# Seven token tiles of 512 and 768 instead of nine of 512

## The chip, the cores and the metric

One core of a Trainium2 chip runs the whole program. The metric is the device time of one execution in microseconds (us), and three runs of the kernel before are at hand. TensorE (PE) multiplies, VectorE (DVE) and ScalarE (ACT) work element by element, GpSimd (POOL) mainly issues stores here, and SyncE's queue (SP) issues the loads.

## What is computed

Linear attention without a mask, a norm over each head's 64 outputs, and a feed-forward layer on all tokens, in float32:

```python
kv = np.einsum('bhsd,bhse->bhde', k, v)            # 8 batches, 8 heads, 576 rows, 64 wide
out = np.einsum('bhsd,bhde->bhse', q, kv)
rms = np.sqrt(np.mean(out * out, axis=-1, keepdims=True) + 1e-06)
x = out / rms * g_norm                             # then 4608 tokens x 512
h = x @ w_in                                       # 512 -> 2048
sp = np.where(h > 20.0, h, np.log1p(np.exp(np.minimum(h, 20.0))))
g = h * np.tanh(sp)                                # Mish
y = g @ w_out                                      # 2048 -> 512
```

## The kernel before

**Numbers.** Each float32 operand of a large product is split into a rounded high part and a rest (`split`: a ScalarE cast, then a VectorE subtraction). A product is three matmuls: high by high, high by rest, rest by high.

**Products.** Both large products use a scheme of seven products on 2 x 2 blocks (a Strassen form, `PROD`). For x @ w_in the blocks are halves of the tokens of a tile, of the 512 inputs and of the 2048 outputs. `x_sum` makes the sums and differences of blocks of x, `x_form` splits the seven left operands ("forms") into fixed rooms, which the products of one tile read and the next tile overwrites.

**Part one.** The 4608 tokens are cut into nine tiles of 512 (`BLOCKS`, `TS`, `OFF`). Tile 0 is multiplied plainly (`whole_group`, line 734), with matmuls of up to 512 columns. Tiles 1 to 8 each have `NQ` = 4 groups, and a group works on two of the eight 128-row chunks of outputs (`chunks`). A group is seven products (slots), and `mm_in` (line 780) gives a product 2 chunks x 2 contraction halves x 3 = 12 matmuls of 256 columns (`TH`). Results lie in PSUM banks "a" and "bc", two of each. ScalarE copies a bank to a room of `u` (`take`, lines 681, 686, 694), the bank is accumulated further two products or more later, VectorE adds it to the copy (`put_in`, line 836), ScalarE applies Mish (line 197), and GpSimd's queue stores g to a DRAM scratch `gd` (line 818), one tensor per tile.

**Attention.** The x of tile j is made while tile j - 1 is multiplied: query loads (452), 32 x 32 transposes on VectorE (470), projection by the key-value product (862, product at 371), squares, sums of squares (532), a table load, logarithm and exponential (542 to 550), a trip of the row scales through DRAM (`keep` 567, `spread` 574) and `normalize` (584).

**w_out.** It comes as raw words; 16 pieces are loaded (224), scaled and joined (215, 210 to 212), differenced and stored to a scratch (`weight_out`), three pieces per tile from tile 2 on. They use two rooms `w64` and two rooms `wx`.

**Part two.** From the last tile's end on, slabs of 256 tokens are loaded from `gd` (`g_load`, 1075), formed, multiplied by w_out (line 1267 for the first slab, 1148 for the others: per product eight matmuls of 512 columns and eight of 256) and stored.

**Order.** Nothing is scheduled automatically. `start(j)` counts slots from tile 0 on, `at(t, f)` puts a step at a slot, and the tables `WHEN`, `LATER` and `LATER0` hold a fractional slot for each step of the attention, the weights and the forms; `LAST` holds those of the change to part two. Steps are emitted in the order of these numbers, and each engine and each queue then works in that order.

Of the kernel before, what the change touches and what calls it, by code (L numbers as in the profile page):

```python
# [8 lines left out]
F32 = mybir.dt.float32  # L9
# [27 lines left out]
def linear_attention_rms_mish_ffn(  # L37
# [47 lines left out]
    TM = max(TS)  # L85
    assert sum(TS) == NTOK
# [12 lines left out]
    def start(j):  # L99
        return FIRST + NS * (j - 1) if j else 0  # L100
    WHEN = {
# [33 lines left out]
    }  # L135
    LATER = {
        "k0": -9, "k1": 0.4878, "k2": 0.2698, "k3": -4, "load0": -20.266, "transpose0": -7.3665,
        "load1": -0.8834, "square0": 1.8552, "scaled0": 1.9552, "transpose1": -0.6728, "square1": 2.0552,
        "scaled1": 2.828, "sums": 5.7127, "table": 6.2457, "ln": 6.6987, "exp": 7.5047, "keep": 7.8047,
# [8 lines left out]
    }  # L148
    LATER0 = {
        "k0": -7, "k1": -2.3472, "k2": -1.299, "k3": -2, "load0": -11, "transpose0": -6, "load1": -5.5,  # L150
        "square0": 5.1305, "scaled0": 0.3, "transpose1": -1, "square1": 0.4, "scaled1": 2.5, "sums": 5.4106,
        "table": 6.6923, "ln": 6.7866, "exp": 7.9866, "keep": 9.0209, "spread": 9.5515, "normalize0": 16.16,
        "normalize1": 17.5, "sum0": 21.4, "sum1": 21.65, "sum2": 22.05, "x0": 25.516, "x1": 25.5, "x2": 26.541,
        "x3": 26.568, "x4": 27.5, "x5": 27.8, "x6": 30.1, "project": 0, "kp": 5.05, "kk": 6,
    }
    LAST = {
# [464 lines left out]
    def x_form(j, f):  # L621

        if j < T32:
            x_sum(j, f)
# [744 lines left out]
```

## Time and profile before

| | |
|---|---|
| median of 3 runs | 808.5 us (807.41 to 808.59) |
| profiled execution, its own time | 809.48 us |
| its span, first to last instruction | 807.7 us |
| mean granted TensorE clock | 0.996 |
| TensorE, VectorE, ScalarE, GpSimd busy | 97%, 74%, 55%, 13% |
| moved by DMA | 158 MB, mean 196 GB/s |

The span is what the trace shows; about 1.8 us of the time lie around it. Durations are in us or ns as marked. A matmul's recorded duration contains pipelining, so that neighbouring matmuls overlap; the distance between the starts of equal matmuls is what one costs in a stream.

### The profile page before, as it was taken

What the parts mean: (1) busy time and instruction counts of PE and PEld (TensorE: products, weight loads), DVE (VectorE), ACT (ScalarE), POOL (GpSimd) and SP (SyncE); (2) the same over time, 40 slices, a digit from 0 to 9 for tenths busy, and PEclk for the clock granted to TensorE, in tenths of its full rate; (3) what the DMA queues carried; (4) which work ended last, traced back from release to release, by engine and by line L of the source; (5) the groups of instructions that cost most, each with busy time, mean ns of one, the idle gap of its engine ahead of it and who ended that gap; (6) DMA issues with size and microseconds to landing.
All of it is one profiled execution on the core that took longest, in us unless ns stands there. A gap on an engine that the chain in (4) does not pass through costs nothing.

```text
span 807.7 us, 16677 instructions
## 1 busy us (share of the span) xinstructions
PE 785.2 (97%) x6764; PEld 716.5 (89%) x6764; DVE 595.2 (74%) x795; ACT 445.4 (55%) x688; POOL 108.5 (13%) x195
## 2 busy tenths in 40 slices
PE   6899999999999988999999999999999999999998
PEld 5777899899999988998999998888888888888887
DVE  3897858575766847676446888888888888878885
ACT  4858776547465754746457654444444444444442
POOL 2210111322322333332111100000000000000000
PEclk9999999999999999999999999999999999999999
DMA  8998468694959757772479923343333334344422
GB/s 294 287 325 245 169 201 290 183 350 130 329 212 290 245 171 241 217 277 102 158 273 337 353 107 131 143 144 130 131 131 131 131 131 141 136 143 143 148 74 54
DMA packets 65453, 158.00 MB, mean 196 GB/s; under 512 B 9184, under 2 KB 29920, under 8 KB 63072
## 3 DMA queue, kind: packets, MB, share of 16 engines
q1 hardware_dynamic: 51136, 109.93, 41.8%
q0 software_dynamic: 14144, 46.93, 15.5%
q8 instruction: 53, 0.87, 0.4%
q14 instruction: 24, 0.20, 0.1%
q10 hardware_dynamic: 96, 0.07, 0.0%
HBM read 100.40 MB, written 56.49 MB: 194 GB/s over the span
## 4 chain that ended last, share of the span: by engine, by line
PE 89%; DMA 4%; DVE 3%; ACT 2%; issue 1%; SPq 1%; ACTq 0%; DVEq 0%
PE a L1148 23%; PE a L780 22%; PE bc L1148 18%; PE bc L780 16%; PE q L1267 2%; DMA w<-in_moe_w_in_dram 2%; PE x L862 2%; PE x L371 2%; DMA fh<-rd 1%; PE a L734 1%; PE x L532 1%; PE bc L734 1%; DMA wfb<-in_moe_w_in_dram 1%; DVE gf L584 0%; PE x L734 0%
## 5 line engine op out<-in xcount | busy, mean ns | idle before, releaser
L200 ACT CAST gf<-g 128x1024 fp32r<-128x1024 f32 (+1 forms) x103 | 105.9, 1044 | 96.1 <-PE a L1148 50.6
L201 DVE TENSOR_TENSOR gf<-g,gf 128x1024 fp32r<-128x1024 f32 (+1 forms) x103 | 123.7, 1214 | 43.9 <-ACT gf L200 43.9
L780 PE MATMUL a<-gf,wfb 128*128 128x256 f32 x1152 | 151.0, 285 | 2.0 <-DVE u L836 2.0
L780 PEld LDWEIGHTS a<-gf,wfb 128*128 128x128 f32 x1152 | 144.3, 194 | 4.2 <-DVE u L836 2.4
L1148 PE MATMUL a<-wfb,gf 128*128 128x512 f32 (+1 forms) x800 | 144.9, 337 | 0.0
L1148 PEld LDWEIGHTS a<-wfb,gf 128*128 128x128 f32 x800 | 125.4, 190 | 16.4
L1148 PE MATMUL bc<-wfb,gf 128*128 128x512 f32 (+1 forms) x544 | 98.0, 337 | 0.0
L1148 PEld LDWEIGHTS bc<-wfb,gf 128*128 128x128 f32 x544 | 82.6, 190 | 10.1
L818 POOL DMA_DIRECT2D gd<-u x96 | 57.1, 597 | 221.1 <-ACT u L197 181.5
L197 ACT ACTIVATE u<-u 128x1024 f32<-128x1024 f32 (+1 forms) x65 | 54.8, 844 | 45.9 <-DVE u L836 45.4
L836 DVE TENSOR_TENSOR u<-bc,u 128x512 f32<-128x512 f32 x64 | 43.3, 687 | 33.5 <-PE bc L780 30.4
L780 PE MATMUL bc<-gf,wfa 128*128 128x256 f32 x384 | 51.8, 284 | 1.3 <-DVE gf L201 0.9
L780 PEld LDWEIGHTS a<-gf,wfa 128*128 128x128 f32 x384 | 48.3, 192 | 5.0 <-issue 4.2
L780 PE MATMUL a<-gf,wfa 128*128 128x256 f32 x384 | 51.9, 284 | 0.0
L780 PE MATMUL bc<-gf,wfb 128*128 128x256 f32 x384 | 51.4, 283 | 0.0
L780 PE MATMUL bc<-a,wfb 128*128 128x256 f32 x384 | 51.4, 283 | 0.0
L780 PEld LDWEIGHTS bc<-gf,wfa 128*128 128x128 f32 x384 | 48.4, 192 | 2.4 <-DVE gf L201 1.1
L1148 PE MATMUL bc<-wfa,gf 128*128 128x256 f32 (+1 forms) x272 | 50.3, 337 | 0.0
L1148 PEld LDWEIGHTS a<-wfa,gf 128*128 128x128 f32 x272 | 44.1, 189 | 6.6
L1148 PE MATMUL a<-wfa,gf 128*128 128x256 f32 (+1 forms) x272 | 49.8, 336 | 0.0
L200 ACT CAST gf<-a 128x1024 fp32r<-128x1024 f32 x17 | 17.9, 1055 | 57.0 <-DVE a L1092 57.0
L780 PEld LDWEIGHTS bc<-a,wfb 128*128 128x128 f32 x384 | 48.4, 192 | 0.6 <-issue 0.6
(203 smaller groups left out, 1183.8 us busy)
## 6 DMA issues: line engine op xcount, KB each, us to landing
g<-gd SPq DMA_DIRECT2D x18, 2048.0 KB
gd<-u POOLq DMA_DIRECT2D x72, 256.0 KB, 4.8
gd<-u POOLq DMA_DIRECT2D x36, 512.0 KB, 6.0
w<-in_moe_w_out_dram SPq DMA_DIRECT2D x32, 256.0 KB
km<-in_k_dram SPq DMA_DIRECT2D x28, 288.0 KB
vm<-in_v_dram SPq DMA_DIRECT2D x28, 288.0 KB
wfb<-in_moe_w_in_dram SPq DMA_DIRECT2D x28, 256.0 KB
out_dram<-u SPq DMA_DIRECT2D x44, 128.0 KB
```

The source lines that it names most:

```text
L197: nc.scalar.activation(o, i, AF.Mish)
L200: nc.scalar.copy(hi, src)
L201: nc.vector.tensor_sub(lo, src, hi.bitcast(F32))
L371: nc.tensor.matmul(outs[a][half(o, a == 1)], kt[half(o), d], vt[half(o), d], start=(c == 0), stop=(c == 8))
L532: nc.tensor.matmul(ss[j][hp * R:(hp + 1) * R, c], sel, sq[j, n][:, a, c], start=True, stop=True)
L734: nc.tensor.matmul(bank[:, h], w[:, a, kc, :], xf[:, h, b, kc, :], start=new and kc == p == 0, stop=(second == 1 and hs[-1] == 1 and kc == ...
L780: nc.tensor.matmul(bank[:, jj], w[:, a, kc, :], xf[:, b, kc, :], start=first and jj == kc == s == 0, stop=(kc == 1 and s == 2), skip_group ...
L818: eng.dma_start(to, o)
L836: nc.vector.tensor_add(o, bank, o)
L862: nc.tensor.matmul(x2[half(o), a, cols], kvt[b % 2][r, m, u], of[r, c, m], start=m == 0, stop=m == 1)
L1148: nc.tensor.matmul(to, of, by, start=first and n == 0, stop=n == len(todo) - 1, skip_group_check=True)
L1267: nc.tensor.matmul(banks[b][:, h], gf[:, a, c, :], wo_form(2 * n + c, right)[:, :, d, :], start=n == c == s == h == 0, stop=last_one, skip ...
```

## The change

Part one has seven tiles: three of 512 tokens and four of 768. Attention runs on parts (`SUBS`): the first three parts are tiles 0 to 2, and then each tile of 768 has two parts of 384 (`TILES`, `HOME`), each with its own steps ("a" and "b" in the tables). In the tiles of 768 a group works on one chunk of outputs instead of two, so that a tile has eight groups and a product six matmuls of 384 columns, in one PSUM bank. All slot numbers in the tables are new. w_out pieces are placed five to a tile over tiles 3 to 5, and the sixteenth after them.

Rooms change with the sizes: the forms' rooms are one tensor (`homes`), `u` is 7 x 384 wide, key and value loads have two rotating rooms and some borrowed ones, `wx` has one room, and one of the two `ow` rooms of part two lies in the room of x. Before the first load of weights its room is now filled with zeros on GpSimd (`clear`). `gd` has rows of 384 in the large tiles, so that a slab there is read in pieces of 256 or 128 tokens per chunk; slabs 0 and 1 are read in four parts each (`g00` to `g13`).

```diff
-    BLOCKS = (16,) * 9
-    NT = len(BLOCKS)
-    TS = [32 * n for n in BLOCKS]
+    SUBS = (512,) * 3 + (384,) * 8
+    TILES = ((0,), (1,), (2,)) + tuple((j, j + 1) for j in range(3, 11, 2))
+    NT = len(TILES)
+    HOME = {j: (i, h if len(js) > 1 else None) for i, js in enumerate(TILES) for h, j in enumerate(js)}
+    SO = [sum(SUBS[:j]) for j in range(len(SUBS))]
+    TS = [sum(SUBS[j] for j in js) for js in TILES]
...
     LATER = {
+        "aload0": -6, "aload1": -5.5, "atranspose0": 3, "atranspose1": 4, "aproject": 5.2, "asquare0": 7.5042,
...
+        "akp": 8.2372, "akk": 14.4383, "asums": 9.5756, "atable": 10.1517, "aln": 10.3517, "aexp": 11.5292,
+        "akeep": 11.7292, "aspread": 12.0958, "anormalize0": 20.8936, "anormalize1": 23.4848, "bload0": 10.3183,
...
+        "bln": 31.5, "bexp": 31.8, "bkeep": 32, "bspread": 33.2, "bnormalize0": 39.266, "bnormalize1": 41.4583,
+        "sum0": 43.3923, "sum1": 45.5101, "sum2": 47.189, "x0": 52.8317, "x1": 52.6366, "x2": 56.3748,
+        "x3": 54.3298, "x4": 56.5377, "x5": 56.9798, "x6": 61.0377, "wload0": 7.7085, "wscale0": 15.8522,
+        "wjoin0": 17.267, "wdiff0": 19.9101, "wblocks0": 20.377, "wforms0": 21.0305, "wstore0": 21.0922,
+        "wload1": 21.2416, "wscale1": 25.1154, "wjoin1": 26.0084, "wdiff1": 26.6154, "wblocks1": 28.0444,
+        "wforms1": 28.1154, "wstore1": 29.2011, "wload2": 27.9154, "wscale2": 33.6, "wjoin2": 34.6151,
+        "wdiff2": 35.1, "wblocks2": 35.366, "wforms2": 36.4421, "wstore2": 36.7421, "wload3": 35.766,
+        "wscale3": 42.3923, "wjoin3": 45.4163, "wdiff3": 45.8813, "wblocks3": 45.9149, "wforms3": 47.1078,
...
+        "wforms4": 65.5, "wstore4": 66.5319, "wload5": 62.5, "wscale5": 67.5, "wjoin5": 69.4963,
...
+        def clear():
+            st["t"] = room()
+            st["w"] = st["t"].rearrange("p b n t -> p (b n) t")
+            nc.gpsimd.memset(st["t"].bitcast(F32), 0.0)
...
+    def bank_of(n, two):
+        def new(name):
+            bank = bank_new(name)
+            return bank[:, :, 0:n] if two else bank.rearrange("p m t -> p (m t)")[:, 0:n].rearrange("p (m t) -> p m t", m=1)
+        return new
...
-        open_pools(wst, ("w64", 2), ("wx", 2), ("wst", 1))
-    at(start(1) + 18, out_pools)
+        open_pools(wst, ("w64", 2), ("wx", 1), ("wst", 1))
+    at(start(3) + 13, out_pools)
...
-        j, n = 2 + min(i, 14) // 3, i % 3 if i < 15 else 3
+        j, n = 3 + min(i, 14) // 5, i % 5 if i < 15 else 5
...
-    def g_load(s):
-        g = gs[s]["g"] = pools["gp"].tile([P, NFC, G], F32, name="g")
-        nc.sync.dma_start(g, gd[s // 2][:, s % 2])
+    def g_load(s, n=None):
...
+        for i in range(NT):
+            th = TS[i] // 2
+            for h in range(2):
+                at_ = OFF[i] + h * th
+                lo, hi = max(at_, s * G), min(at_ + th, (s + 1) * G)
+                if lo < hi:
+                    to, of = g[:, :, lo - s * G:hi - s * G], gd[i][:, h, :, lo - at_:hi - at_]
...
+                    nc.sync.dma_start(to, of)
...
-        for n in range(NQ):
-            st = {"i": i, "n": n, "chunks": (2 * n, 2 * n + 1), "bank": bank_new, "take": nc.vector.tensor_copy if T32 <= i < NT - 1 and n in BY_DVE else nc.scalar.copy}
+        two = i == 0 or TS[i] < TM
+        for n in range(NQ if two else NF2):
+            st = {"i": i, "n": n, "chunks": (2 * n, 2 * n + 1) if two else (n,), "bank": bank_new if i == 0 else bank_of(TS[i] // 2, two), "take": nc.scalar.copy}
```

## Rows read from the trace of the kernel before

**Rows 1.** The page, busy time of each engine with its share of the span and its instructions:

```profile
PE 785.2 (97%) x6764; PEld 716.5 (89%) x6764; DVE 595.2 (74%) x795; ACT 445.4 (55%) x688; POOL 108.5 (13%) x195
```

**Rows 2.** Stretches of the span: start and end, length, then for PE, PEld, DVE, ACT and POOL the busy time with its instructions, the granted clock, the DMA engines' share, GB/s. The start, two windows of the 512-token tiles, part two:

```profile
0.00:36.00 36.00, 27.69 (x286) 22.09 (x287) 18.93 (x34) 22.22 (x41) 8.11 (x31) 0.95 0.90 300
...
184.00:232.00 48.00, 48.00 (x572) 46.19 (x572) 32.85 (x53) 29.35 (x49) 12.57 (x21) 1.00 0.77 255
...
280.00:328.00 48.00, 43.13 (x508) 40.36 (x507) 31.34 (x57) 25.81 (x47) 16.79 (x25) 0.96 0.63 208
...
472.00:805.00 333.00, 332.01 (x1914) 293.05 (x1912) 272.15 (x265) 152.79 (x187) 0.00 (x0) 1.00 0.36 123
```

**Rows 3.** The same view for the matmuls of line 780 alone (PE, then PEld), from the start of tile 3 to the end of tile 8:

```profile
178.90:455.00 276.10, 247.11 (x2018) 244.18 (x2017) 0.99 0.69 234
```

**Rows 4.** Timeline of TensorE at the end of tile 0: start, duration to the end of the last, instructions, tile shape and count:

```profile
73.44 2.88 PE L734 MATMUL a<-gf,wfb 128*128 128x512 f32 x12
76.16 2.88 PE L734 MATMUL bc<-gf,wfb 128*128 128x512 f32 x12
78.88 2.88 PE L734 MATMUL a<-gf,wfb 128*128 128x512 f32 x12
81.60 2.88 PE L734 MATMUL bc<-gf,wfb 128*128 128x512 f32 x12
84.32 1.59 PE L780 MATMUL a<-gf,wfb 128*128 128x256 f32 x12
```

**Rows 5.** The chain that ended last, in a tile of part one and in a slab of part two: start, share of the chain, what:

```profile
209.18 2.88 PE bc L780 x24
...
505.67 5.56 PE a L1148 x32
```

**Rows 6.** Groups of instructions by line and shape: count, busy us, mean ns of one, idle before them and what ended it. Copies, Mish, casts, adds, subtractions, the table load and the stores of g:

```profile
L201 DVE TENSOR_TENSOR gf<-g,gf 128x1024 fp32r<-128x1024 f32 x102 | 123.2, 1221 | 43.4 <-ACT gf L200 43.4
L200 ACT CAST gf<-g 128x1024 fp32r<-128x1024 f32 x102 | 105.5, 1050 | 96.1 <-PE a L1148 50.6 <-DVE g L1097 31.1 <-DVE g L1095 14.4
...
L818 POOL DMA_DIRECT2D gd<-u x96 | 57.1, 597 | 221.1 <-ACT u L197 181.5 <-issue 13.1 <-ACT kv L393 6.4
...
L836 DVE TENSOR_TENSOR u<-bc,u 128x512 f32<-128x512 f32 x64 | 43.3, 687 | 33.5 <-PE bc L780 30.4 <-ACT u L197 1.5 <-ACT fa L503 1.2
...
L197 ACT ACTIVATE u<-u 128x1024 f32<-128x1024 f32 x32 | 34.0, 1062 | 8.8 <-DVE u L836 8.3
...
L200 ACT CAST gf<-gf 128x512 fp32r<-128x512 f32 x36 | 21.8, 620 | 1.8 <-PE a L780 1.2 <-DVE gf L584 0.6
L197 ACT ACTIVATE u<-a 128x512 f32<-128x512 f32 x35 | 21.1, 602 | 1.6 <-DMA gd<-u 1.6
...
L681 ACT COPY u<-a 128x512 f32<-128x512 f32 x32 | 18.7, 585 | 30.9 <-PE a L780 29.3 <-ACT gf L200 1.5
...
L542 ACT ACT_TABLE_LOAD x8 | 10.3, 1283 | 0.1
```

**Rows 7.** Stretches again (columns as in rows 2): the last group of tile 2, in which the forms of tile 3 are made:

```profile
168.90:179.00 10.10, 10.10 (x87) 10.10 (x86) 6.33 (x11) 6.84 (x12) 2.65 (x5) 1.00 0.97 325
```

**Rows 8.** Stretches again: tile 4, then tile 5, from first product to first product of the next tile:

```profile
224.85:270.79 45.94, 45.94 (x555) 44.13 (x554) 32.50 (x55) 28.02 (x48) 11.07 (x19) 1.00 0.76 252
270.79:324.15 53.36, 48.49 (x554) 45.83 (x553) 35.25 (x61) 30.65 (x54) 19.45 (x29) 0.97 0.62 205
```

**Rows 9.** Timeline of TensorE in tile 5; in brackets the idle time before and what ended it:

```profile
285.02 0.45 PE L371 MATMUL x<-vm,km 64*64 64x64 f32 x13 [2.58 <-issue]
...
313.93 2.41 PE L780 MATMUL a<-gf,wfb 128*128 128x256 f32 x10 [1.77 <-DVE u L836]
```

**Rows 10.** The chain that ended last, at the entry to tile 1 and in tile 5: start, share, what:

```profile
74.63 4.68 DMA fh<-rd
...
299.92 5.67 DMA fh<-rd
```

**Rows 11.** What SP's queue waited for between 270 and 320 us: total us, times, longest:

```profile
SPq L224 <- DMA wod<-w: 24.2, 3, 13.3
```

**Rows 12.** What the engines waited for over the whole span, the normalize line: total us, times, longest:

```profile
DVE gf L584 <- DMA fh<-rd: 7.2, 5, 2.4
```

**Rows 13.** Timeline of ScalarE (the exponential of tile 1's row scales), then of SP's queue (their store and the spread):

```profile
70.21 0.63 ACT L550 ACTIVATE fl<-fl 128x512 f32<-128x512 f32 x1
...
70.87 1.18 SPq L567 DMA_DIRECT2D rd<-fl  x4
...
73.96 1.28 SPq L574 DMA_DIRECT2D fh<-rd  x2
```

**Rows 14.** Timeline of the first us: GpSimd's memsets and loads, and the first weight load on SP's queue:

```profile
1.28 0.20 POOL L913 MEMSET wfa<- 128x128 f32 x1
...
1.95 0.14 POOL L917 MEMSET sel<- 128x32 f32 x1
...
2.31 1.38 SPq L242 DMA_DIRECT2D w<-in_moe_w_in_dram  x2
2.33 1.20 POOL L925 DMA_DIRECT2D gcol<-in_g_norm_dram  x2
```

**Rows 15.** DMA issues by kind: count, KB each, median us from issue to landing. Stores that read a `w64` room and a `wx` room:

```profile
wod<-w POOLq DMA_DIRECT2D x16, 256.0 KB, 3.2
...
wod<-wx POOLq DMA_DIRECT2D x16, 128.0 KB, 3.8
```

More of the change, by code (lines that the diff above doesn't have):

```diff
@@ L148, in linear_attention_rms_mish_ffn @@
     }
     LATER0 = {
[L150 to L154, printed above, removed]
+        "aload0": -14, "aload1": -12.6004, "atranspose0": -6.6293, "atranspose1": -4.5, "aproject": -3.5,
@@ L381, in linear_attention_rms_mish_ffn @@
     open_pools(wst, ("w64", 1), ("wd", 1))
-    first = fq.tile([P, 2 * TM], F32, name="a22")[:, 0:2 * NKC * D].rearrange("p (s n d) -> p s n d", s=2, d=D)
+    first = spare[:, 0:2 * NKC * D].rearrange("p (s n d) -> p s n d", s=2, d=D)
     kvn, kvy = first[:, 0], first[:, 1]
@@ L525, in sums @@
                 return
-            if j >= T32:
-                ss[j] = x2_new()[:, 0]
-                for c in (slice(0, T),):
-                    for n in range(2):
-                        for a in range(2):
-                            hp = 2 * n + a
-                            nc.tensor.matmul(ss[j][hp * R:(hp + 1) * R, c], sel, sq[j, n][:, a, c], start=True, stop=True)
-                return
-            ss[j] = ps_t.tile([P, T], F32, name="ss")
+            ss[j] = x2_new()[:, 0, 0:tj]
             for n in range(2):
@@ L603, in x_rows, with x_home @@
     def x_rows(j, u):
-        return x_of(j).rearrange("p h a n -> p a h n")[:, 2 * u:2 * u + 2]
-    def x_sum(j, f):
-        a11, a12, a21, a22 = block(j, 0, 0), block(j, 1, 0), block(j, 0, 1), block(j, 1, 1)
-        n = TS[j]
+        i, h = HOME[j]
+        if h is None:
+            return x_of(i).rearrange("p h a n -> p a h n")[:, 2 * u:2 * u + 2]
+        return x_of(i)[:, h, 2 * u:2 * u + 2]
+    PAIRS = ((A11, A21), (A12, A22), (S1, S2))
+    def x_home(f):
+        pair = next(n for n, p in enumerate(PAIRS) if f in p)
+        n = PAIRS[pair].index(f)
+        return homes[:, (4 * pair + 2 * n) * TM:(4 * pair + 2 * n + 2) * TM]
@@ new lines, in x_sum @@
+    def x_sum(i, f):
+        a11, a12, a21, a22 = block(i, 0, 0), block(i, 1, 0), block(i, 0, 1), block(i, 1, 1)
+        n = TS[i]
+        if n == TM:
+            room = att.tile([P, 2 * T], F32, name={S1: "fa", S2: "fh", S4: "fl"}[f])
+        else:
+            if f == S1:
+                xsums[i] = pools["wd"].tile([P, 4, 2 * P], F32, name="wd").rearrange("p a n -> p (a n)") if i == 2 else x_room
+            room = spare if f == S2 else xsums[i]
+        xsums[i, f] = room[:, 0:n].rearrange("p (c n) -> p c n", c=2)
@@ L785, in linear_attention_rms_mish_ffn, with u_room @@
     held = []
-    u_all = up.tile([P, 7 * T], F32, name="u")
     u_uses = {}
-    def u_room(name, small, n):
-        first, size, bufs = {
-            ("la", False): (0, T, 2), ("lb", False): (2 * T, T, 1), ("r", False): (3 * T, 2 * T, 2),
-            ("la", True): (0, TM // 2, 3), ("lb", True): (3 * TM // 2, TM // 2, 2), ("r", True): (3 * T, TM, 3),
-        }[name, small]
-        k = u_uses[name, small] = u_uses.get((name, small), -1) + 1
+    def u_room(name, i, n):
+        k = u_uses[name] = u_uses.get(name, -1) + 1
+        if name == "o":
+            return u_all[:, k % 2 * 2 * T:][:, 0:n]
+        if TS[i] < TM:
+            if "more" not in u_uses:
+                u_uses["more"] = pools["w64"].tile([P, 4, 2 * P, 2], U32, name="w64").rearrange("p a b c -> p (a b c)").bitcast(F32)
+            more = u_uses["more"]
+            room = {
+                ("la", 0): u_all[:, 2 * T:], ("la", 1): more[:, 3 * T:], ("lb", 0): more[:, 2 * T:], ("lb", 1): more[:, 2 * T:],
+                ("r", 0): u_all, ("r", 1): more,
+            }[name, k % 2]
+            return room[:, 0:n]
+        first, size, bufs = {"la": (0, TF, 2), "lb": (2 * TF, TF, 1), "r": (3 * TF, TM, 2)}[name]
         return u_all[:, first + k % bufs * size:][:, 0:n]
@@ L840, in put_in @@
             done(right, st["r"], None, 3, 2)
-    units = {j: [unit_steps(j, u) for u in range(2)] for j in range(NT)}
+    units = {j: [unit_steps(j, u) for u in range(2)] for j in range(len(SUBS))}
     def do(j, u, *steps):
@@ L979, in linear_attention_rms_mish_ffn @@
         at(t, steps[name])
-    def soon(j, name):
-        return (LATER0 if j == 2 else LATER)[name]
-    for b in range(4, B):
-        t = start(b - 2)
-        at(t + soon(b - 2, "kp"), lambda b=b: k_product(b))
-        at(t + soon(b - 2, "kk"), lambda b=b: k_keep(b))
-        for p in range(4):
-            at(t + soon(b - 2, f"k{p}"), lambda b=b, p=p: k_load(b, p))
+    KP = {3: 4, 5: 5, 6: 6, 8: 7}
     def attention(j):
+        i, h = HOME[j]
+        t, table = start(i - 1), LATER0 if i == 3 else LATER
         def spread():
@@ L994, in spread @@
             units[j][1]["spread"]()
-        units[j][0]["spread0"] = spread
-        t = start(j - 1)
         def when(name, f):
-            at(t + soon(j - 1, name), f)
+            at(t + table["ab"[h] + name], f)
         for u in range(2):
@@ L1007, in attention @@
         when("spread", spread)
-        for n, f in enumerate((S1, S2, S4)):
-            when(f"sum{n}", lambda f=f: x_sum(j, f))
-        for n, f in enumerate(MADE):
-            when(f"x{n}", lambda f=f: x_form(j, f))
-    for j in range(3, NT):
+        if j in KP:
+            b = KP[j]
+            when("kp", lambda: k_product(b))
+            when("kk", lambda: k_keep(b))
+            for p in range(4):
+                when(f"k{p}", lambda p=p: k_load(b, p))
+        if h:
+            for n, f in enumerate((S1, S2, S4)):
+                at(t + table[f"sum{n}"], lambda f=f: x_sum(i, f))
+            for n, f in enumerate(MADE):
+                at(t + table[f"x{n}"], lambda f=f: x_form(i, f))
+    for j in range(3, len(SUBS)):
         attention(j)
@@ L1179, in o_store @@
                 at_ = st["s"] * G + r * P + n * R
-                i = max(i for i in range(NT) if OFF[i] <= at_)
-                b, s0, seg = next(e for e in segments(i) if e[2].start <= at_ - OFF[i] < e[2].stop)
-                runs.setdefault((i, b), []).append((r, b * S + s0 + (at_ - OFF[i] - seg.start) // R, (seg.stop - seg.start) // R))
+                j = max(j for j in range(len(SUBS)) if SO[j] <= at_)
+                b, s0, seg = next(e for e in segments(j) if e[2].start <= at_ - SO[j] < e[2].stop)
+                runs.setdefault((j, b), []).append((r, b * S + s0 + (at_ - SO[j] - seg.start) // R, (seg.stop - seg.start) // R))
             for rs in runs.values():
@@ L1206, in pair_rooms @@
         if n == 0:
-            return [pools["g0"].tile([P, m, 2, 2, P], F32R, name=f"g{m}") for m in (4, 3)]
-        return [gf_room() for _ in range(2)]
+            a, b = [pools["g0"].tile([P, m, 2, 2, P], F32R, name=f"g{m}") for m in (4, 3)]
+            return [(a, b)[f // 4][:, f % 4] for f in range(7)]
+        at_ = {
+            1: {A11: 0, S1: 4, A12: 8, A22: 12, S2: 24, S3: 28, S4: 32},
+            2: dict(zip(range(7), (16, 20, 36, 40, 44, 48, 52))),
+            3: dict(zip(range(7), range(56, 84, 4))),
+        }[n]
+        return [homes[:, at_[f] * P:(at_[f] + 4) * P].bitcast(F32R).rearrange("p (s c n) -> p s c n", s=2, c=2) for f in range(7)]
     t8 = start(NT - 1)
@@ L1213, in linear_attention_rms_mish_ffn @@
     for s in range(2):
-        at(t8 + LAST[f"g{s}"], lambda s=s: g_load(s))
+        for n in range(NQ):
+            at(t8 + LAST[f"g{s}{n}"], lambda s=s, n=n: g_load(s, n))
     rooms0 = {}
```

171 lines of the change are left out of this document (85 added, 86 removed), and 87 rows, old and new, of tables (LAST, LATER, WHEN).

## The prediction

> **What bounds the kernel now.** I read the totals first: TensorE is busy for 785.2 of 807.7 us, and VectorE and ScalarE stand at 74% and 55% [rows 1]. Busy shares alone don't decide, so the stretches come next. In the stage of the 512-token tiles TensorE is busy for all 48.00 of 48.00 us at a granted clock of 1.00, and in the second half of the kernel for 332.01 of 333.00 [rows 2]; VectorE and ScalarE have 15 to 19 us of slack in such a 48 us window. TensorE is therefore the bound, and a change pays there only by giving it fewer or shorter instructions, or by removing a stall. One stall is large: the window 280 to 328 has only 43.13 busy and a clock of 0.96 [rows 2]. The start is different: up to 36 us the DMA engines are 90% busy at 300 GB/s [rows 2], and TensorE idles for 8.3 us.
>
> **What a matmul costs.** The recorded duration (283 ns) overlaps its neighbours, so I take distances between starts. In the chain 24 matmuls of 256 columns take 2.88 us: 120.0 ns each [rows 5]. In tile 0 twelve matmuls of 512 columns start every 2.72 us (73.44, 76.16, 78.88, 81.60, 84.32): 226.7 ns each [rows 4]. The line through both has 0.4168 ns per column, 2.4 GHz, and 13.3 ns per matmul whatever its width. For 384 columns it gives 173.3 ns. A second reading: in the second half 32 matmuls, half of 512 and half of 256 columns, take 5.56 us [rows 5], so 512 columns are 227.5 and 384 are 173.8.
>
> **The change part by part.**
>
> *Matmuls.* Tiles 3 to 8 of before hold 6 x 4 x 7 x 12 = 2016 matmuls of 256 columns (2018 in their window, edges included [rows 3]). After, the same tokens are 4 tiles x 8 groups x 7 products x 6 = 1344 matmuls of 384 columns: the same columns, 672 fixed parts fewer. 2016 x 120.0 = 241.9 us; 1344 x 173.3 = 232.9. **-9.0 us** (-8.4 by the second reading), all of it on the path. The Trainium skill (TensorE: Matmul & The Clock Gate, Back-to-back issue gap) gives an isolated warm matmul N/2.4 + 2.5 ns: by that only 672 x 2.5 = 1.7 us would be won, an estimate that speaks against the change. The trace disagrees: 120.0 ns at 256 columns is 13.3 over the columns' own time, so I keep -9.0.
>
> *The stall in tile 5.* Tile 4 takes 45.94 us and tile 5, with one TensorE instruction less, 53.36 [rows 8]: 7.4 us lost. TensorE waits 2.58 us inside the key-value product and 1.77 us for the add of line 836 [rows 9]; the lower clock after these holes is the rest. Its cause is in SP's queue: the w_out load of line 224 waits up to 13.3 us for a room whose stores haven't landed [rows 11], the spread of line 574 stands behind it, and the normalize of line 584 waits for that transfer, 5.67 us in the chain [rows 10], with the adds behind it. The diff places every one of these steps anew (w_out pieces five to a tile over tiles 3 to 5, loads 7 to 23 slots apart, a slot now 6 x 173.3 = 1.04 us). Between a piece's store and the load that takes its room again lie at least 6.6 slots, 6.9 us, against 3.2 us from issue to landing of such a store [rows 15] and three to five issues of some 0.6 us. I count the stall as gone: **-7.4 us** (0 if it comes back).
>
> *Less cover for each eviction.* A product lasts 1.04 us instead of 1.44, so the two products between an accumulator's copy and its next use shrink from 2.88 to 2.08 us. Per group, with sizes scaled between rows 6: ScalarE 3 copies of 478 ns, two Mish of 495 and one of 847, 3.3 us; VectorE 3 adds of 554, 1.7 us; the group lasts 7.28. In general that fits. At the entry to a 768 tile it doesn't: seven casts of 835 ns bring ScalarE to 9.1 us, seven subtractions of 954 ns bring VectorE to 8.3, where before a whole such group used 6.84 and 6.33 of 10.1 us [rows 7]. The cover: each form has 6 products, 6.2 us, between its last use and its next, and needs about 1.9, so 4 us of lag are free. If that cover were gone, the excess of 1.8 us would reach TensorE at the three entries whose last group is already of 384 columns: 0 to 5.5. I take half, **+2.7**.
>
> *The spread.* From the end of the exponential to the arrival of the first spread rows the trace has 70.84 to 79.31, 8.5 us [rows 10, 13]. Planned now: 9.36 slots (9.7 us) in a tile's first part, but 7.47 slots (7.8 us) in its second, 0.6 of which is the exponential itself. So four normalizes are about 1.3 us late, and the adds queue behind each on VectorE. Even before, five such waits came to 7.2 us [rows 12]. 0 to 5.2, half of it hidden by the 2.08 us: **+2.6**.
>
> *One wx room instead of two.* ScalarE's scale of a w_out piece now waits until the stores that read the last piece have landed: two issues of 0.6 us and 3.8 us to landing [rows 15], 5 us. The plan leaves 4.1 slots (4.3 us) for the second piece of a tile, 5.3 and more for others, and 2 slots for the last piece. Behind the scale on ScalarE stand the copies that TensorE needs. Late by 0.7 three times and 2.9 once, 0 to 5: **+1.7**.
>
> *Attention in eight parts of 384 instead of six of 512.* Batch borders cut both into 11 pieces, so projections, query loads and their DMAs stay equal. Two more pairs of table loads (1283 ns each [rows 6]) fall on ScalarE, eight more row-scale stores and eight more spreads on SP, 24 more stores of 597 ns [rows 6] on POOL's queue, which was 13% busy [rows 1]. Hidden: 0.
>
> *Start.* A memset of 2048 columns now precedes the first weight load. Memsets of 32 and 128 columns took 0.14 and 0.20 us [rows 14]: some 1.5 us, from about 3.5 to 5.0, and SP's first weight load moves from 2.31 to 5.0, with what is queued behind it. The 1.7 MB of query, key and value ahead of it keep the DMA engines full for some 5.5 us at 300 GB/s, so I take 0; +2.7 if that cover fails, -1.5 if the keys come sooner for it.
>
> *g scratch in four parts, rows of 1 KB or 512 B instead of 16 KB (16 chunks x 256 tokens x 4 bytes).* The second half moves a mean 123 GB/s at a DMA share of 0.36 [rows 2]: 0.
>
> **Sum** against the profiled execution's 809.5 us (span 807.7): 809.5 - 9.0 - 7.4 + 2.7 + 2.6 + 1.7 = 800.1. The median of the runs, 808.5, is 1.0 lower, so the forecast is **799 us**.
>
> **The rivals.**
> - *No new stall.* The tables place each step apart, and the window 184 to 232 of before ran without one [rows 2]. The last three terms vanish, the start may give 1.5: 790.6 to 793. Against it: the shorter slots.
> - *In-order queues become the bound; slower.* Place: ScalarE and VectorE in the 32 groups of 384 columns. ScalarE had 29.35 of 48 us busy, VectorE 32.85 [rows 2], with four groups, one attention part and three w_out pieces in about that time. With eight smaller groups, two smaller parts and five pieces I estimate about 51 us each in some 65 us (58.2 of products and 7 of attention): 78%, in queues where a copy stands behind a cast or a table load. It decides from 16.4 us of new stalls, 0.51 us per group. At 0.7 per group, 22.4 us: 814.5.
> - *The tile-5 stall comes back at full size elsewhere*, by SP's order: 799 + 7.4 = 806.4.
> - *The change doesn't shorten the matmuls.* If the fixed part grew with width, 384 columns would cost 180 ns and the term would be 0: 808. Rows 4 speak against it (512 would be 240). By the gap that the Trainium skill states (same section) 1.7 us would be won, 806.3.
>
> **How the numbers follow.** Forecast, 795 to 804, 0.52; no new stall 0.18; slower queues 0.13; stall back 0.12; no shorter matmuls 0.05. A measurement of this kernel tells 0.2%, 1.6 us, from no change: faster is below 806.9, slower above 810.1. Faster 0.52 + 0.18 + 0.07 + 0.02 = 0.79; same 0.04 + 0.03 = 0.07; slower 0.13 + 0.01 = 0.14. The range runs from the full gain, 790, to 809, which takes in the returned stall and the unshortened matmul and leaves out the slower case and little below: some 0.83. The likeliest case alone has 795 to 804: 3.5 to 12 us of new stalls out of 15.7 at most.
>
> **What would show it.** Right: 384-column matmuls in the 768 tiles, 6 in 1.04 us; a tile of about 58.2 us plus some 7 to 8 us of attention; full TensorE in windows inside a tile; holes of 0.3 to 2 us only at tile entries, at line 584's counterpart and behind the scale of w_out pieces. The second half stays at 333 us and the first 84 us within 3. Wrong: 384 columns at 180 ns; TensorE holes in most groups, released by the adds or copies; a clock below 1.00 in the 768 tiles; a later first matmul.

## The result, and the profile after

The changed kernel is slower: a median of 816.8 us (815.0 to 819.1, four runs) beside 808.6 us of the kernel before, timed with it, a ratio of 1.0103 (95% interval 1.0067 to 1.0139). The forecast was 799 us, faster. The profiled execution took 819.08 us with a span of 817.3; it is the slowest of the four, so the losses read from it below are at the upper end.

The totals show little. Busy times of the page, then stretches (columns as in [rows 2]): a window of the first 768-token tile, one that covers most of the third and the start of the last, and part two.

```profile
PE 788.6 (96%) x6108; PEld 709.2 (87%) x6108; DVE 595.1 (73%) x809; ACT 457.4 (56%) x737; POOL 125.0 (15%) x220
...
184.00:232.00 48.00, 45.24 (x577) 39.44 (x576) 23.81 (x41) 24.78 (x45) 10.73 (x18) 0.93 0.71 228
...
345.00:420.00 75.00, 67.58 (x384) 62.74 (x384) 47.82 (x85) 40.53 (x75) 30.91 (x50) 0.96 0.66 218
472.00:805.00 333.00, 333.00 (x1938) 294.87 (x1937) 274.54 (x268) 157.38 (x194) 0.00 (x0) 1.00 0.43 130
```

Part two is as before [rows 2]. Tile 1 starts at 84.27 us (84.32 before), part two's first slab at 460.45 (450.40 before). So tiles 1 to 6 take 376.2 us instead of 366.1, where the forecast has 366.1 - 9.0 - 7.4 + 7.0 = 356.7: all of the miss, 19.5 us, lies there.

The matmuls did become cheaper. Timeline of TensorE in the first 768-token tile, to hold beside [rows 4]:

```profile
251.15 2.24 PE L805 MATMUL a<-gf,wfb 128*128 128x384 f32 x12
253.23 2.24 PE L805 MATMUL bc<-gf,wfb 128*128 128x384 f32 x12
255.31 1.20 PE L805 MATMUL a<-gf,wfa 128*128 128x384 f32 x6
```

Twelve take 2.08 us from start to start, 173.3 ns each, and many groups without attention last exactly 42 x 173.3 ns = 7.28 us. The loss is not spread over the groups; a few are long. From the starts of their first matmuls: group 3.3 (the fourth of tile 3) has 15.82 us, its counterpart 4.3 with the same work 10.00; 5.5 has 11.85 and 6.2 has 11.73 instead of 7.28. Beside undisturbed groups with the same work, groups 4.7 to 5.7 lose 11.2 us in sum, 6.2 loses 4.5, 3.3 loses 5.8, the entry to tile 3 (2.3 and 3.0) 2.6: 24 us, of which the forecast had 7. The remaining 2.4 us of the miss are about what the attention's own instructions add (an estimate): a part of 512 tokens adds 3.26 us to its group (the first of tile 7 before: 13.34 instead of 10.08), a part of 384 adds 2.72 (group 4.3), and eight of these are 2.2 us more than six of those. In the long groups TensorE waits (timeline, in brackets the idle time and what ended it; before had two such waits, [rows 9]):

```profile
213.34 2.29 PE L805 MATMUL a<-gf,wfb 128*128 128x384 f32 x6 [2.56 <-DVE u L868]
...
351.24 0.96 PE L805 MATMUL a<-gf,wfb 128*128 128x384 f32 x4 [1.39 <-ACT u L212]
...
378.64 1.31 PE L805 MATMUL bc<-gf,wfb 128*128 128x384 f32 x6 [1.88 <-ACT u L711]
...
417.17 2.28 PE L805 MATMUL a<-gf,wfb 128*128 128x384 f32 x7 [2.61 <-DVE u L868]
```

Two of the four are followed by a half-clock stretch, and in one it begins during the wait. The windows with a granted clock of 0.50 (1.2 GHz) in tiles 1 to 6 add up to 13.7 us; before had one of 3.41:

```profile
212.80:219.63 6.83, 6.29 (x74) 5.02 (x75) 2.49 (x5) 2.33 (x4) 0.67 (x1) 0.50 0.71 259
380.05:383.47 3.42, 3.42 (x13) 3.42 (x12) 2.85 (x4) 0.00 (x0) 1.12 (x2) 0.50 0.98 351
417.60:421.02 3.42, 3.42 (x13) 3.42 (x12) 0.47 (x2) 0.87 (x2) 1.95 (x3) 0.50 0.64 198
```

What held TensorE up stands on ScalarE and two queues. ScalarE (timeline): two evictions wait for the store of an older product to land, because their room of `u` is the one it reads, and the scale of the sixteenth w_out piece (line 230) waits with the copies behind it. The view names no releaser for that one; the last store that reads the one `wx` room had been issued at 408.49 and landed at 413.92:

```profile
350.70 0.49 ACT L212 ACTIVATE u<-a 128x384 f32<-128x384 f32 x1 [3.45 <-DMA gd<-u]
...
378.11 0.48 ACT L711 COPY u<-bc 128x384 f32<-128x384 f32 x1 [3.94 <-DMA gd<-u]
...
414.07 0.66 ACT L230 ACTIVATE wx<-w 128x512 f32<-128x512 f32 x1 [3.80 <-issue]
```

The product stores that the first two wait for (line 850) are late because they stand in POOL's queue behind the five stores (350 to 354) of a piece of chunk 4 or 5. From the first to the end of the last these take 8.3 us here, and 7.4 to 8.4 us over the four pieces:

```profile
365.11 0.76 POOL L350 DMA_DIRECT2D wod<-w  x1
365.86 0.56 POOL L351 DMA_DIRECT2D wod<-wx  x1
367.86 0.71 POOL L352 DMA_DIRECT2D wod<-wx  x1 [1.44 <-issue]
369.51 0.78 POOL L353 DMA_DIRECT2D wod<-wst  x1 [0.94 <-ACT u L719]
372.62 0.75 POOL L354 DMA_DIRECT2D wod<-w  x1 [2.32 <-DVE wx L226]
373.36 1.27 POOL L850 DMA_DIRECT2D gd<-u  x2
```

The fifth store comes 2.30 to 2.36 us late in each of the four pieces. The releaser named is "issue" once and three different lines of VectorE, which speaks against any of these as the cause. In tile 3 it is SP's queue: sixteen query loads stand ahead of the row-scale store (`rd<-fl`), though the exponential had ended at 199.4.

```profile
194.23 8.80 SPq L480 DMA_DIRECT2D qs<-in_q_dram  x16
203.13 1.13 SPq L584 DMA_DIRECT2D rd<-fl  x4
205.49 1.27 SPq L591 DMA_DIRECT2D fh<-rd  x2
...
206.15 5.62 DMA fh<-rd
```

(The last line is of the chain, as [rows 10]; the spread landed at 211.77.) The normalize waits for it, an add waits behind the normalize, and TensorE for the add at 213.34.

### The profile page after: what moved, and what is told of

Read it like the earlier page. It is cut to its first block, busy times and chain, and to the rows that moved or that the text cites. A ratio compares the mean times of both kernels' runs of the same rounds, so it can differ in the third digit from the quotient of the medians.

```text
span 817.3 us, 15626 instructions
## 1 busy us (share of the span) xinstructions
PE 788.6 (96%) x6108; PEld 709.2 (87%) x6108; DVE 595.1 (73%) x809; ACT 457.4 (56%) x737; POOL 125.0 (15%) x220
## 4 chain that ended last, share of the span: by engine, by line
PE 74%; DMA 12%; issue 5%; ACT 3%; DVE 3%; POOL 2%; SPq 1%; POOLq 0%; ACTq 0%; DVEq 0%
PE a L1184 23%; PE bc L1184 17%; PE a L805 15%; PE bc L805 10%; DMA wfb<-in_moe_w_in_dram 4%; PE q L1314 2%; DMA w<-in_moe_w_out_dram 2%; PE x L894 2%; PE x L404 2%; DMA vm<-in_v_dram 1%; PE bc L759 1%; DMA wfb<-in_v_dram 1%; ACT L212 1%; DMA fa<-rd 1%; POOL gd L850 1%
## 5 line engine op out<-in xcount | busy, mean ns | idle before, releaser
L805 PE MATMUL a<-gf,wfb 128*128 128x384 f32 (+1 forms) x864 | 156.9, 327 | 10.6 <-DVE u L868 7.1
L805 PE MATMUL bc<-gf,wfb 128*128 128x384 f32 (+1 forms) x576 | 96.7, 318 | 1.9 <-ACT u L711 1.9
L805 PEld LDWEIGHTS bc<-gf,wfb 128*128 128x128 f32 x576 | 90.8, 189 | 3.9 <-ACT u L711 2.2
L1184 PEld LDWEIGHTS bc<-wfb,gf 128*128 128x128 f32 x544 | 82.6, 190 | 10.1
L868 DVE TENSOR_TENSOR u<-bc,u 128x384 f32<-128x384 f32 (+1 forms) x72 | 40.6, 568 | 58.2 <-PE bc L805 53.7
L215 ACT CAST gf<-x 128x1024 fp32r<-128x1024 f32 (+3 forms) x48 | 40.1, 840 | 56.1 <-DVE x L1128 55.4
L212 ACT ACTIVATE u<-u 128x768 f32<-128x768 f32 (+2 forms) x75 | 52.0, 697 | 25.6 <-DVE u L868 25.3
L216 DVE TENSOR_TENSOR gf<-x,gf 128x1024 fp32r<-128x1024 f32 (+3 forms) x48 | 46.0, 959 | 10.0 <-ACT gf L215 9.6
L805 PE MATMUL a<-gf,wfa 128*128 128x384 f32 (+1 forms) x288 | 52.7, 323 | 0.0
L805 PE MATMUL bc<-gf,wfa 128*128 128x384 f32 (+1 forms) x288 | 51.9, 319 | 0.8 <-DVE gf L216 0.8
L1184 PEld LDWEIGHTS bc<-wfa,gf 128*128 128x128 f32 x272 | 43.0, 190 | 5.7
```

What stands on the lines that cost most here:

```text
L212: nc.scalar.activation(o, i, AF.Mish)
L215: nc.scalar.copy(hi, src)
L216: nc.vector.tensor_sub(lo, src, hi.bitcast(F32))
L805: nc.tensor.matmul(bank[:, jj], w[:, a, kc, :], xf[:, b, kc, :], start=first and jj == kc == s == 0, stop=(kc == 1 and s == 2), skip_group ...
L868: nc.vector.tensor_add(o, bank, o)
L1184: nc.tensor.matmul(to, of, by, start=first and n == 0, stop=n == len(todo) - 1, skip_group_check=True)
```

## Experiments

The theory after this reading: the gain of 9 us is real and a few long waits eat it (A). The rivals: the slots are too short everywhere (B), or the single wx room is the main cost (C); D to H are named as they come. Ratios are to the kernel before, timed beside each.

**no_prep.** The steps of a w_out piece between load and store are skipped, and the store is one transfer (two for chunks 4 and 5) of 7 x 128 words per partition:

```diff
-                conv["out", i][s]()
+                if s in (0, 6):
+                    conv["out", i][s]()
```

> Left out of the computation: the preparation of w_out in part one. Each of the sixteen pieces still loads as many bytes into its room (of q, in place of w_out) and is stored from there (one or two stores on the POOL queue), but its scale, join, differences, blocks and forms are gone, so part two multiplies g by something that is not w_out. Theory A (a few long waits at the pieces: the one wx room, five stores in a row ahead of a product store, SP held by the w64 rooms): the five waits of tiles 5 and 6 go (1.39, 0.47, 0.59, 1.88 and 2.61 us, in sum 6.9) and the two half-clock stretches behind them with about 1.7 us each, so 806 to 807 us; the 2.56 us wait of tile 3 at 213 us stays as it is. Rival B (the slots are too short for the evictions everywhere): every group gains, those of tiles 3 and 4 too, and the time goes to 798 to 802.

829.9 us, 1.0229 (1.0177 to 1.0281): slower, against both theories. Its POOL queue shows why. A piece of another chunk, stored in 128 rows of 3584 B, then one of chunk 4, the same bytes per store in 896 rows of 512 B:

```profile
281.94 0.55 POOL L352 DMA_DIRECT2D wod<-w  x1
282.73 0.54 POOL L848 DMA_DIRECT2D gd<-u  x1 [0.24 <-issue]
...
316.41 1.01 POOL L352 DMA_DIRECT2D wod<-w  x1 [2.72 <-issue]
320.87 1.00 POOL L352 DMA_DIRECT2D wod<-w  x1 [3.45 <-issue]
324.86 1.86 POOL L848 DMA_DIRECT2D gd<-u  x3 [2.99 <-issue]
```

The first form costs POOL 0.55 us and no hold. The second costs 1.0 us and holds the queue for 2.0 to 4.5 us ahead of and behind each store, and TensorE then waited 4.96, 5.55 and 4.85 us for products' rooms. Bytes and queue are the same; the row length differs. The Trainium skill (DMA: Bandwidth & Descriptors, Anatomy of one DMA, SWDGE path) calls descriptor generation small and says that "You can emit a lot of descriptors before the incremental cost shows up". Here a cost shows at 896 rows in a store; no run separates the making of descriptors for short rows from their writing.

**raw_all, spread_first, both.** raw_all stores chunks 4 and 5 like the others (half the bytes, 3 rows of the scratch per partition and piece instead of 14), splits them in the last tile, and uses the room that this frees as a second wx room. spread_first moves half of the query loads behind the spread.

```diff
-    RAW = (0, 1, 2, 3, 6, 7)
+    RAW = (0, 1, 2, 3, 4, 5, 6, 7)
...
-        open_pools(wst, ("w64", 2), ("wx", 1), ("wst", 1))
+        open_pools(wst, ("w64", 2), ("wx", 2))
...
-        "bload1": 11.6958,
+        "bload1": 12.3,
```

> The four w_out pieces of chunks 4 and 5 are stored as the others are (three stores, no split in part one) and split in the last tile instead; the room that held their split forms becomes a second room for the scaled words (wx). Theory A: the waits at 349, 370, 373 and 378 us (products waiting for a u room whose store stood behind five piece stores) and the one at 414 us (the scale waiting for the single wx room) go, with the half-clock stretches behind the last two: 807 to 810 us, the 2.56 us wait at 213 us unchanged. Rival B (the same work in the same short slots): the work only moves from tiles 5 and 6 to the last tile, 815 to 817 us.

> One number: the second half of the query loads of an attention part (8 of 16 loads on the SP queue) is issued behind the store and the spread of the row scales instead of ahead of them. Theory A: the row-scale store leaves SP some 4 us sooner, the normalize in group 3 of tile 3 no longer waits for the spread, and the 2.56 us wait at 213 us goes with most of its 6.83 us half-clock stretch: 811 to 813 us. Rival B: 816 to 817 us, the wait moves to the next eviction in the queue.

> The edits of raw_all and spread_first together. Theory A: the gains add, 802 to 806 us, below the kernel before. Rival B: 815 to 817 us.

raw_all: 808.1 us, 0.9979 (0.9960 to 0.9997), as theory A has it: groups 4.7 to 5.7 now lose under 2 us, 6.2 still 2.1. spread_first: 815.8, 1.0078 (1.0051 to 1.0106), 1 us instead of 4 to 6 and not clear of the noise beside the changed kernel (1.0067 to 1.0139): the store of the scales left sooner, but now the transposes waited for the later query loads, and a wait of 1.49 us stood at 212 us in the projection. both: 807.7, 0.9978 (0.9955 to 1.0001). The gains do not add.

**long_rows, raw_wx1, before_rows.** They separate the parts of raw_all. long_rows changes only the order of the scratch of chunks 4 and 5, so that the same five stores write rows of 512 to 2048 B (5 per partition and piece); with it each load of these chunks in the last tile becomes two; before_rows does this in the kernel before; raw_wx1 is raw_all with one wx room.

```diff
-    wod = [tc.dram_tile([P, 2, 7, P] if c in RAW else [P, 2, 7, 2, P], ...
+    wod = [tc.dram_tile([P, 2, 7, P] if c in RAW else [P, 2, 2, 7, P], ...
```

> Nothing but the order of w_out's scratch is changed: the pieces of chunks 4 and 5 still make five stores of the same bytes, but in rows of 512 to 2048 B instead of 512 B throughout (5 rows per partition and piece instead of 14). In the kernel without the preparation of w_out, a 448 KB store in 128 rows of 3584 B cost the POOL queue 0.54 us and no wait, and one of 896 rows of 512 B 1.0 us and then a hold of 2.7 to 4.5 us. Theory A (the rows of those four pieces hold the POOL queue, the product stores behind them land late, and Mish and the copies wait for their rooms): the waits at 349, 370, 373 and 378 us go and with them 7 to 9 us: 808 to 810 us; the wait of the scale for the wx room (414 us) and the one at 213 us stay. Rival B (the bytes, or the five issues, or the work beside them): 815 to 817 us.

> raw_all with one room for the scaled words again, so that the three-store form of the pieces of chunks 4 and 5 is tried without the second wx room. Theory A (the rows in the POOL queue): 808 to 811 us, nearly all of raw_all's gain of 8.7 us, with only the wait of the scale in tile 6 back (2.6 us and its half-clock stretch). Rival C (the single wx room was the main cost): 813 to 816 us.

> The kernel before with the scratch order of long_rows (same stores, same bytes, rows of 512 to 2048 B). Theory A: the holds ahead of the fifth store of those pieces (2.31, 2.32 and 3.80 us there) go, the w_out loads get their rooms sooner, and part of the 7.4 us stall of tile 5 goes: 803 to 806 us. Rival B: 808 to 810 us, no change.

long_rows: 812.4 us, 1.0048 (1.0029 to 1.0067). The hold is gone; the five stores of this piece take 3.7 us, those of all four 3.3 to 4.7, and where a store still comes late it follows the engine that makes its data:

```profile
361.74 0.54 POOL L350 DMA_DIRECT2D wod<-w  x1 [1.76 <-ACT w L215]
363.00 0.54 POOL L351 DMA_DIRECT2D wod<-wx  x1 [0.72 <-DVE wx L216]
363.66 0.72 POOL L352 DMA_DIRECT2D wod<-wx  x1
364.37 0.56 POOL L353 DMA_DIRECT2D wod<-wst  x1
364.92 0.54 POOL L354 DMA_DIRECT2D wod<-w  x1
```

In the profiled execution groups 4.7 to 5.7 lose 4.6 us instead of 11.2. The gain of 4.4 us in the medians is half of what theory A promised. raw_wx1: 812.9, 1.0049 (1.0023 to 1.0075), between A and C: the second room is worth 0.7% by the ratios. The two profiled executions show less (spans 808.6 and 806.6, and 1.5 of these 2.0 us lie before tile 1, where the kernels do not differ); in group 6.2, where the last scale stands, the room is worth 2.1 us (11.46 and 9.35). before_rows: 804.2 us, **0.9949 (0.9930 to 0.9967)**, and in its profiled execution tile 5 takes 48.4 us instead of 53.4. So the short rows cost the kernel before as much as the changed one; they explain the waits, not the difference between the two kernels.

**before_wx1, before_raw.** One part of the change done alone (one wx room in the kernel before), and raw_all's stores in the kernel before.

> The kernel before with one room for the scaled words of a w_out piece instead of two: one part of the change done alone. Theory C (the second room is worth as much in both kernels): between raw_wx1 (1.0049 of the kernel before) and raw_all (0.9979) the second room made 0.7%, so here 812 to 815 us. Theory D (the room costs only where the pieces come as closely as the plan of the new tiles puts them, the last one above all): 808 to 810 us, no change.

> The kernel before with the pieces of chunks 4 and 5 in the three-store form and split in the last tile (the edit of raw_all; it has two wx rooms as it is). Long rows alone brought this kernel 4.2 us. Theory A (the rows in the POOL queue are what this edit removes): 802 to 805 us, as with long rows. Rival (the splits moved to the last tile cost there what is won): 807 to 810 us.

before_wx1: 822.4 us, 1.0155 (1.0121 to 1.0188), more than theory C has. Every third scale waits, and TensorE at its worst 3.47 us behind it (ScalarE, then TensorE). The view names a query load there; the last store that reads the room landed at 318.94:

```profile
303.97 0.67 ACT L215 ACTIVATE wx<-w 128x512 f32<-128x512 f32 x1
...
319.01 0.66 ACT L215 ACTIVATE wx<-w 128x512 f32<-128x512 f32 x1 [6.26 <-DMA qs<-in_q_dram]
...
320.19 2.93 PE L780 MATMUL a<-gf,wfa 128*128 128x256 f32 x12 [3.47 <-ACT u L694]
```

With one room the third scale of a tile followed 13.1 to 15.0 us after the second (10.8 in the last case), where two rooms had let it follow after 7.6 to 8.9. The changed kernel's new plan spreads most of the pieces: two scales wait long there (5.02 us at 384.79, 3.80 at 414.07), and TensorE waits behind the second. before_raw: 810.3, 1.0016 (1.0000 to 1.0033): in its trace tiles 1 to 8 take 358.7 us instead of 366.1, as much less as the tile-5 stall [rows 8], but part two takes 366.9 instead of 357.3. What the stores gave, the splits put late took back: in the last group TensorE waits 6.98 us for an add that stands behind them on VectorE, with 10.24 us at half clock.

**no_prep_raw, no_pieces.** What raw_all still loses through w_out: no_prep_raw leaves out its arithmetic and makes its three stores of a piece one, no_pieces leaves out the loads too (the one store then reads q).

> Left out of the computation: the preparation of w_out in part one, as in no_prep, but every piece is stored from its load room with one store of 128 rows of 3584 B, and the splits of all eight chunks stand in the last tile as in raw_all. Beside raw_all (808.1 us) it tells what the pieces' scale, join, differences and stores cost now, with the loads unchanged. Theory E (what is left lies in tile 3, in the entries and in the last tile, with no part of the pieces in it): 804 to 807 us, the gaps at 179, 182, 194, 212, 224 to 226 and 444 us all there. Rival B (ScalarE and VectorE too dense in the short slots): 795 to 800 us, those gaps gone too.

> Left out of the computation: everything of w_out in part one but the write of its scratch. Each of the sixteen pieces is one transfer of 448 KB from q to the scratch on the POOL queue; SP has no w_out loads in part one, ScalarE and VectorE no work on the pieces. Theory F (the w_out loads on SP hold up the key and value loads of tile 3): the waits of the key-value products go, as in no_prep_raw they did not (805.7 us), 798 to 801 us. Theory G (tile 3 has too many loads of its own for the attention): the waits at 194 and 224 to 230 us stay, 803 to 806 us.

no_prep_raw: 805.7 us, 0.9963 (0.9934 to 0.9992), as theory E says. Rival B, short slots everywhere, falls: without any work on the pieces tile 3 keeps its gaps, up to 2.40 us in group 3.4. Only the one at 212 us, which theory E had kept, is gone. Beside raw_all the gain, 1.3 us by the ratios, is not clear of the noise. no_pieces: 803.8, 0.9916 (0.9886 to 0.9947), inside G's range by its median: the key-value products no longer wait (0.18 us), but the add behind the normalize does, longer than ever:

```profile
215.19 2.29 PE L800 MATMUL a<-gf,wfb 128*128 128x384 f32 x6 [5.33 <-DVE u L863]
```

**raw_wlate, one_q, q_split.** Tile 3 by itself. raw_wlate is raw_all with its second to fourth piece 4.4, 2 and 1.6 slots later; one_q also makes the sixteen query loads of the tile's second part two transfers of the same bytes in rows twice as long; q_split, also built on raw_wlate, issues every second query load from POOL's queue.

> raw_all, and in the first 768-token tile alone the second, third and fourth w_out pieces 4.4, 2 and 1.6 slots later, so that no key or value load stands behind a w_out load that waits for its room. Theory F (SP's order behind those w_out loads makes the waits of the key-value product at 224 to 228 us): the 4.4 us that group 3.4 loses in raw_all go, 803 to 805 us. Theory G (the transfers themselves or the rooms are late): 807 to 809 us, the waits stay.

> raw_wlate with the sixteen query loads of one attention part, the second one prepared in the first 768-token tile, made as two transfers of the same 768 KB in all, of other rows of q than the reference's (so the outputs of that part's tokens are not the reference's). SP then issues 2 transfers there instead of 16 (some 9 us). Theory H (SP's issue time for the query loads ahead of the row-scale store and the spread is what makes group 3.3 wait for the normalize): the 3.2 us lost there in raw_wlate (a wait of 1.90 us at 215.7 us and a half-clock stretch of 3.41 us) go and no other wait takes their place: 804 to 806 us. Theory G (the bytes on the DMA engines are late, whoever issues them): 808 to 810 us.

> raw_wlate with every second query load of the attention parts from tile 4 on issued by the POOL queue instead of SP: all of the computation, SP's sixteen issues become eight. Theory H: SP reaches the row-scale store some 4.5 us sooner, most of the 3.2 us lost in group 3.3 goes, and the store and spread of the later tiles come sooner too: 804 to 807 us. Rival (POOL's product stores stand behind the eight query loads, their rooms come late): 809 to 813 us, with waits of Mish or the copies for stores of products.

raw_wlate: 808.9 us, 0.9978 (0.9958 to 0.9998), no gain over raw_all: group 3.4 loses 1.3 us now instead of 4.2, but 3.3 has a wait of 1.90 us for the normalize and a half-clock stretch. one_q: 805.4, 0.9948 (0.9930 to 0.9966), by theory H. SP issues two loads, the scales leave at once (the exponential ends at 198.82), and that wait is gone with its half-clock stretch:

```profile
193.58 0.95 SPq L475 DMA_DIRECT2D qs<-in_q_dram  x2
198.85 1.15 SPq L587 DMA_DIRECT2D rd<-fl  x4
```

The bytes were the same and the store left as soon as its data stood, so SP's issue time is shown to be the cause of this one wait. Part of the gain went again: a key-value product waits 2.10 us at 224 us. The Trainium skill (DMA: Bandwidth & Descriptors, Issuing engines are not separate DMA queues) says that issuing from several engines saves only issue time, "usually small relative to the DMA itself". Here sixteen issues add up to 8.80 us ahead of a transfer of 5.62 us. q_split: 807.5, 0.9977 (0.9954 to 1.0000), inconclusive. Its profiled execution (804.7 us) has no wait over 0.3 us in groups 3.3 and 3.4, but its twelve runs lie between 804.1 and 814.2.

**v3, v4, v5, v6.** Several steps moved at a time, to see whether single waits add up.

> raw_all and spread_first, and four steps moved: the sixteenth piece of w_out from slot 62.5 to slots 47 to 52 of its tile; in the second half of a tile the second query transpose, the projection and what follows 0.9 to 1.1 slots later; the key-value product there 1.6 slots later; the last two splits of the last tile 2 slots later. Theory A (single waits make up the rest): of the waits left in the kernel with both edits, 1.26 us (213 us), 2.3 us with a half-clock stretch (228 us), 1.4 us (412 us) and 1.1 us (446 us) go, some 7 us: 799 to 803 us. Rival B: each moved step waits or makes another wait, 806 to 809 us.

> raw_all and spread_first, and three moves: in tile 3 the loads of the second to fourth w_out pieces come 4.4, 2 and 1.6 slots later, so that the key and value loads no longer stand behind a w_out load that waits for its room (3.3 us on SP at 215 us); in tile 2 the second attention part comes 1.1 to 2.3 slots earlier; the last two splits come 2 slots later. Theory E: the 2.3 us wait of the key-value product at 228 us with its half-clock stretch, the two waits of 0.75 us at 181 and 184 us and the 1.1 us at 447 us go: 801 to 804 us. Rival B: 807 to 809 us, as without the moves, the waits taking other places.

> raw_wlate with three more single steps: the key-value product of a tile's first half 2.8 slots later, the load of the sixth w_out chunk in the last tile 2.6 slots sooner (ahead of the split that waits for it), and the first load of g behind the second w_out load instead of ahead of it. Theory F: the 1.3 us at 194 us, the wait at 445 us (1.1) and the one at 410 us (1.6, a product store that needs 8.9 us to land beside loads of 640 and 512 KB) go too: 799 to 803 us, below the kernel before. Theory G: 806 to 809 us.

> q_split with two of its remaining single waits undone: the fourth w_out piece of the first 768-token tile back at its planned slot (a wait of 1.19 us at 247 us), and the first load of g behind the second w_out load (1.41 us at 406 us, a product store beside loads of 640 and 512 KB). Theory H (the waits left are single and separate): 803 to 805 us, faster than the kernel before by 0.6 to 0.9%. Rival: 807 to 808 us as q_split, the waits taking other places.

v3: 814.9 us, 1.0074 (1.0050 to 1.0098); v4: 811.1, 1.0013 (0.9988 to 1.0037); v5: 810.9, 1.0011 (0.9994 to 1.0029). Each removed the waits it aimed at in part and made others: v5's key-value product no longer waits, and a product waits 3.00 us at 215.00 in its place. v6: 805.8, **0.9965 (0.9943 to 0.9986)**: the two waits that it aimed at are gone, and the key-value product waits 1.12 and 2.55 us in tile 3 instead. It beats the kernel before and the changed one (by 1.3%), not before_rows.

## Why the prediction was wrong, point by point

- **Matmuls, -9.0.** Right: 173.3 ns, and undisturbed groups of 7.28 us.
- **The stall of tile 5, -7.4.** This step failed. I put it down to SP's order at the room `w64` [rows 11], priced the stores behind it at some 0.6 us an issue and 3.2 us to landing [rows 15], and concluded that 6.9 us of distance would do. The five stores of a piece of chunks 4 and 5 occupy POOL's queue for 7.4 to 8.4 us, so product stores and rooms are late, and SP's w_out loads still wait for a room's stores (up to 12.2 us between 300 and 400 us). Longer rows alone took 4.9 of the 7.4 us out of tile 5 in the kernel before (before_rows); before_raw, which also moves the splits away, took all of it. The changed kernel keeps those stores, and groups 4.7 to 5.7 lose 11.2 us, 4.6 with longer rows. This is the rival "comes back elsewhere", of which I had the price but not the cause. Why it cost more than before is argued, not shown: a room of `u` with no second one (that of block 21) comes round after 7.28 us where it had 10.1, a cover that I never costed.
- **The spread, +2.6.** The term was mis-sized, and a queue left out. I compared the planned distance with the 8.5 us trip of tile 1, in which SP had nothing ahead. In tile 3 it had 8.80 us of query loads, and from the exponential's end to the landing passed 12.4 us (199.4 to 211.77); for 3.8 of these the store stood behind the loads. Group 3.3 lost 5.8 us.
- **One wx room, +1.7.** The place and the wait were right (the sixteenth piece, 2.9 us late by my estimate, 3.80 measured); what I left out was the half-clock stretch behind it, so that group 6.2 lost 4.5. With a second room it still loses 2.1, behind the late product store of the last section, so 2.1 to 2.4 us of it are the room's. Alone in the kernel before the room costs 13.8 us.
- **Less cover at the entries, +2.7.** The size came out by luck, the place did not: the entry to tile 3, which I had left out, loses 2.6 us (two waits of 0.75 us for the subtractions of the forms); those to tiles 4 to 6 lose nothing in raw_all. In the changed kernel itself group 4.7 loses 1.5 us, which goes with raw_all's stores.
- **Attention in eight parts, 0.** Wrong twice. TensorE's own work for eight parts is about 2 us longer than for six (estimate above). And in tile 3 two key-value products are made, whose loads share rooms and SP's queue with the queries: from raw_all on this tile takes between 72.4 us (q_split) and 82.1 us (no_prep_raw) in the profiled executions, 76.7 in the changed kernel, whichever wait was removed.
- **Start and g scratch, 0.** Right: a memset of 1.81 us, first load of weights at 5.36 us, tile 1 at 84.27; part two has 333.00 of 333.00 us busy.
- **The rival "in-order queues, slower"** (0.13) named the right family and the wrong place: not 0.5 us in each of 32 groups, but three clusters, two of them on the queues of POOL and SP, which I had at 13% and at no price. That its 814.5 us lies near the result is luck.

Settled are the short rows (4.4 us here by the medians, 4.2 in the kernel before), SP's issue time ahead of the spread (2.4 us by the ratios of raw_wlate and one_q, 3.5 by their medians), and that the w_out arithmetic in short slots is not the bound. Not settled is the last 6 to 7 us between v6 and the forecast. Waits in tile 3 changed place in five kernels; that SP, its rooms and the landing times form one chain there is my reading, argued from this, not shown by one run.

## What to carry to other kernels

Price a queue by what stands in it ahead of the step you need, in issues and in rows, not by its busy share: 8.8 us of loads on SP and 8.3 us of five stores on POOL decided here at 15% POOL busy. When a tile grows, work out for each single-buffered room how much time its old content has to land. Before placing an old stall's cause by its releaser, compare like instructions: waits of always 2.3 us with changing releasers pointed to the queue itself here, and the longer rows confirmed it.

## What was not expected of the hardware

- A store of 448 KB from POOL's queue costs 0.55 us in 128 rows of 3584 B, and 1.0 us plus a hold of 2.0 to 4.5 us in 896 rows of 512 B; with rows of up to 2 KB the fifth store's delay of 2.3 us goes.
- A wait of TensorE of 1.4 to 3 us came with a half-clock stretch of 3.41 or 6.83 us in some places and with none in others (in the kernel before [rows 9] 1.77 us at 313.93 with one and 2.58 us at 285 without, in one_q 2.10 us without). The spread of the runs differs as well: q_split's cover 10.1 us, those of before_rows 1.8 (803.7 to 805.5). That such waits cause the spread is a guess.
- A product store of 384 columns took 9.02 us to land in raw_all's last tile beside loads of 640 and 512 KB; the median of its kind in that run is 3.4 us:

```profile
400.03 9.02 DMA gd<-u
```
